# Sliding-window attention and soft mixture of experts on one core: a rewrite with grouped q/k rows, subtracted row maxima, a fixed pipeline of head pairs and column-tiled experts

## The chip, the core and the metric

The kernel runs on one core of a Trainium2 chip (trn2). The core has a matrix engine (TensorE, PE in the profile; its weight loads stand under PEld), a vector engine (DVE), a scalar engine (ACT), GpSimd (POOL) and a queue for transfers (SP). Transfers between the chip's memory (HBM) and the core's SBUF run on 16 DMA engines. Matmul results land in PSUM, which has 8 banks of 2 KB for each of 128 partitions. The metric is the device time of one execution in microseconds (us); the number that counts is the median of several runs.

## The reference

Two stages in a row. Eight batches of eight heads, 576 positions, 64 channels:

```python
scores = scale * np.matmul(q, k.transpose(0, 1, 3, 2))
rel = pos[:, None] - pos[None, :]
mask = (rel >= 0) & (rel < 64)
scores = np.where(mask, scores, -1000000000.0)
scores = scores - np.max(scores, axis=-1, keepdims=True)
attn = np.exp(scores)
attn = attn / (np.sum(attn, axis=-1, keepdims=True) + 1e-09)
out = np.matmul(attn, v)                      # becomes x: 4608 rows of 512
```

Each position sees itself and the 63 positions before it. Then a soft mixture with 32 slots, four for each of 8 experts (512 -> 1024 -> 512):

```python
logits = x @ phi                              # 4608 x 32
d = np.exp(logits - logits.max(0)); d /= d.sum(0) + 1e-09
slot_input = d.T @ x                          # 32 x 512, sums over all 4608 rows
h = np.maximum(slot_input[e] @ w1[e], 0.0)    # 4 rows of each expert
slot_out[e] = h @ w2[e]
c = np.exp(logits - logits.max(1, keepdims=True)); c /= c.sum(1, keepdims=True) + 1e-09
return c @ slot_out                           # 4608 x 512, float32
```

No expert can start before every batch's attention is done, since `slot_input` sums over all rows.

## The kernel before

The work is done in fp16 with fp32 sums. It goes through one loop over the batches `b` and, inside, over four pairs of heads `hp`; a scheduler of the framework orders the instructions of each engine by their dependencies.

Loading: q, k and v of a batch come by GpSimd's queue, each as five transfers (one for each 128 positions, lines 212 and 219), a row of 64 channels being a run of its own: 256 bytes of fp32 in HBM, 128 bytes of fp16 in SBUF. The buffers `q_bf`, `k_bf`, `v_aug`, `v_shf` exist twice. `v_shf` is a copy of `v_aug` moved by 64 positions, made by two transfers within SBUF from SP's queue (lines 223 and 226); the blocks of 64 queries with even index need it, because their 128 keys straddle two of `v_aug`'s groups.

A head pair: `stage_tr` turns q and k so that channels lie on partitions, with plain matmuls against an identity (lines 97 to 109), and ACT and DVE move the results to `qT` and `kT` (lines 105, 106, 111, 112). `stage_qk` multiplies 9 blocks of 128 keys with 64 queries for each head (line 122); ACT takes the exponential with the scale (lines 126 to 129), with no maximum subtracted, and DVE multiplies with a 0/1 mask (lines 127, 130). `stage_av` multiplies with v and a column of ones (lines 146, 148), whose result is the sum of the row; DVE divides (lines 151, 152) into `x_b`. It runs one pair late, from the list `pending`.

Mixture, front: `moe_front_a` and `moe_front_b` for the batch before run at the second and third pair: x is transposed (line 164), multiplied with phi (173, 175), put through the exponential without a maximum (177, 178), transposed back (185) and multiplied with x (198); DVE adds the result to `slotnum`. The exponentials themselves stay in `dnumT`; one over each row's sum stays in `crcp`.

Experts: weights of five experts fit at a time; loads of experts 0 to 4 are issued after batches 3 to 7, and experts 5 to 7 are loaded inside the expert loop, as buffers come free. Each expert has eight 512-column matmuls with four rows of slots (line 276), a rectifier, eight small transposes (285) and eight 512-column matmuls into `sop` (291). Every expert writes to the same low partitions of PSUM.

Output: for each group of 128 rows one matmul (line 301), ACT or DVE with the scale `crcp` (303, 306) into one of two buffers `ob`, and one large and one small transfer a batch (309, 311).

Of the kernel before, what the change touches and what calls it, by code (L numbers as in the profile page):

```python
# [13 lines left out]
AXX = mybir.AxisListType.X  # L14


@with_exitstack
def kernel(
# [15 lines left out]
    SPE = NSLOT // E  # L34
    NB = S // 64
    NC = (S + 127) // 128
    NHD = D // 128
    NFC = F // 128
    scale = 1.0 / float(Dh) ** 0.5

    const = ctx.enter_context(tc.tile_pool(name="const", bufs=1))
    psum = ctx.enter_context(tc.tile_pool(name="psum", bufs=8, space=bass.MemoryType.PSUM))
    pin = ctx.enter_context(tc.tile_pool(name="pin", bufs=2))
    pw = ctx.enter_context(tc.tile_pool(name="pw", bufs=4))
    pxb = ctx.enter_context(tc.tile_pool(name="pxb", bufs=2))
    pxt = ctx.enter_context(tc.tile_pool(name="pxt", bufs=4))
    pmo = ctx.enter_context(tc.tile_pool(name="pmo", bufs=1))
    pex = ctx.enter_context(tc.tile_pool(name="pex", bufs=5))
    pet = ctx.enter_context(tc.tile_pool(name="pet", bufs=2))
    pou = ctx.enter_context(tc.tile_pool(name="pou", bufs=2))  # L50

    ident_f = const.tile([128, 128], FP32, name="ident_f")
    make_identity(nc, ident_f)
    ident_h = const.tile([128, 128], FP16, name="ident_h")
    make_identity(nc, ident_h)

    mask0 = const.tile([128, 64], FP16, name="mask0")
    nc.gpsimd.memset(mask0, 1.0)
    nc.gpsimd.affine_select(
        out=mask0, in_=mask0, compare_op=ALU.is_ge, fill=0.0,  # L60
        base=-1, pattern=[[-1, 64]], channel_multiplier=1,
    )
    nc.gpsimd.affine_select(
        out=mask0, in_=mask0, compare_op=ALU.is_ge, fill=0.0,
        base=64, pattern=[[1, 64]], channel_multiplier=-1,
    )
    mask_bA = mask0[:, :].unsqueeze(1).broadcast_to([128, 4, 64])
    mask_bB = mask0[:, :].unsqueeze(1).broadcast_to([128, 5, 64])

    phi_sb = const.tile([128, NHD, NSLOT], FP16, name="phi_sb")  # L70
    nc.gpsimd.dma_start(out=phi_sb, in_=moe_phi.rearrange("(c p) s -> p c s", p=128))

    dnumT = pmo.tile([32, B, S], FP16, name="dnumT")
    dsums = pmo.tile([32, B + 1], FP32, name="dsums")
    slotnum = pmo.tile([32, D], FP32, name="slotnum")
    slot_inT = pmo.tile([128, NHD, NSLOT], FP16, name="slot_inT")
    slot_oa = pmo.tile([32, D], FP16, name="slot_oa")
    crcp = pmo.tile([128, B, NC], FP32, name="crcp")
    dinv = pmo.tile([32, 1], FP32, name="dinv")

    w1_t = {}
    w2_t = {}

    def load_expert(e):
        w1s = pex.tile([128, NHD, F], FP16, name="w1s", tag="w1s")
        w2s = pex.tile([128, NFC, D], FP16, name="w2s", tag="w2s")
        nc.gpsimd.dma_start(out=w1s, in_=moe_w1[e].rearrange("(c p) f -> p c f", p=128))  # L87
        nc.gpsimd.dma_start(out=w2s, in_=moe_w2[e].rearrange("(c p) d -> p c d", p=128))
        w1_t[e] = w1s
        w2_t[e] = w2s  # L90

    def stage_tr(b, hp, q_bf, k_bf, small):
        h0 = 2 * hp
        qT = pw.tile([128, S], FP16, name="qT", tag="qT")
        kT = pw.tile([128, 64 + S], FP16, name="kT", tag="kT")
        nc.vector.memset(kT[:, 0:64], 0.0)
        nc.tensor.matmul(small[:, 0, :], q_bf[0:64, 4, h0:h0 + 2, :], ident_h[0:64, 0:64],
                         start=True, stop=True)
        nc.tensor.matmul(small[:, 1, :], k_bf[0:64, 4, h0:h0 + 2, :], ident_h[0:64, 0:64],
                         start=True, stop=True)  # L100
        tq = psum.tile([128, 512], FP32, name="tq", tag="ps")
        for c in range(4):
            nc.tensor.matmul(tq[:, 128 * c:128 * c + 128], q_bf[:, c, h0:h0 + 2, :],  # L103
                             ident_h[:, :], start=True, stop=True)
        nc.scalar.copy(out=qT[:, 512:576], in_=small[:, 0, :])  # L105
        nc.scalar.copy(out=qT[:, 0:512], in_=tq[:, :])  # L106
        tk = psum.tile([128, 512], FP32, name="tk", tag="ps")
        for c in range(4):
            nc.tensor.matmul(tk[:, 128 * c:128 * c + 128], k_bf[:, c, h0:h0 + 2, :],  # L109
                             ident_h[:, :], start=True, stop=True)  # L110
        nc.vector.tensor_copy(out=kT[:, 576:640], in_=small[:, 1, :])
        nc.vector.tensor_copy(out=kT[:, 64:576], in_=tk[:, :])  # L112
        return qT, kT

    def stage_qk(qT, kT, small):
        pms = []
        for hl in range(2):
            r0 = 64 * hl
            sA = psum.tile([128, 8, 64], FP32, name="sA", tag="ps")
            for i in range(NB):  # L120
                dst = sA[:, i, :] if i < 8 else small[:, 2 + hl, :]
                nc.tensor.matmul(dst, kT[r0:r0 + 64, 64 * i: 64 * i + 128],  # L122
                                 qT[r0:r0 + 64, 64 * i: 64 * i + 64],
                                 start=True, stop=True)
            pmt = pw.tile([128, NB, 64], FP16, name="pmt", tag="pmt")
            nc.scalar.activation(pmt[:, 0:4, :], sA[:, 0:4, :], AF.Exp, scale=scale)  # L126
            nc.vector.tensor_tensor(out=pmt[:, 0:4, :], in0=pmt[:, 0:4, :], in1=mask_bA, op=ALU.mult)  # L127
            nc.scalar.activation(pmt[:, 4:8, :], sA[:, 4:8, :], AF.Exp, scale=scale)  # L128
            nc.scalar.activation(pmt[:, 8, :], small[:, 2 + hl, :], AF.Exp, scale=scale)
            nc.vector.tensor_tensor(out=pmt[:, 4:9, :], in0=pmt[:, 4:9, :], in1=mask_bB, op=ALU.mult)  # L130
            pms.append(pmt)
        return pms

    def stage_av(b, hp, pms, v_aug, v_shf, x_b):
        for hl in range(2):
            h = 2 * hp + hl
            pmt = pms[hl]
            av = psum.tile([128, 512], FP32, name="av", tag="ps")
            avv = av[:, 0:NC * 65].rearrange("p (c x) -> p c x", x=65)
            for i in range(NB):  # L140
                if i % 2 == 1:
                    rhs = v_aug[:, h, (i - 1) // 2, 0:65]
                else:
                    rhs = v_shf[:, h, i // 2, 0:65]
                r0b = 64 * (i % 2)
                nc.tensor.matmul(av[r0b: r0b + 64, 65 * (i // 2): 65 * (i // 2) + 65],  # L146
                                 pmt[:, i, :], rhs, start=True, stop=True)
            nc.tensor.matmul(av[64:128, 65 * 4: 65 * 4 + 65], pmt[:, 8, :],  # L148
                             v_aug[:, h, 0, 0:65], start=True, stop=True)
            rc = pw.tile([128, NC], FP32, name="rc", tag="rc")  # L150
            nc.vector.reciprocal(rc[:, 0:NC], avv[:, 0:NC, 0])  # L151
            nc.vector.tensor_tensor(  # L152
                out=x_b[:, 0:NC, 64 * h: 64 * h + 64], in0=avv[:, 0:NC, 1:65],
                in1=rc[:, 0:NC].unsqueeze(2).broadcast_to([128, NC, 64]), op=ALU.mult)

    def moe_front_a(b, x_b):
        smx = psum.tile([128, NHD, 64], FP32, name="smx", tag="ps")
        xTs = []
        for kk in range(NHD):
            tx = psum.tile([128, 512], FP32, name="tx", tag="ps")  # L160
            for c in range(NC):
                pn = 128 if c < 4 else 64
                dst = tx[:, 128 * c:128 * c + 128] if c < 4 else smx[:, kk, :]
                nc.tensor.matmul(dst, x_b[0:pn, c, 128 * kk: 128 * kk + 128],  # L164
                                 ident_h[0:pn, 0:pn], start=True, stop=True)
            xT = pxt.tile([128, S], FP16, name="xT", tag="xT")
            nc.scalar.copy(out=xT[:, 0:512], in_=tx[:, :])  # L167
            nc.scalar.copy(out=xT[:, 512:576], in_=smx[:, kk, :])
            xTs.append(xT)
        ltA = psum.tile([128, 512], FP32, name="ltA", tag="ps")  # L170
        ltB = psum.tile([128, 64], FP32, name="ltB", tag="ps")
        for kk in range(NHD):
            nc.tensor.matmul(ltA[0:32, :], phi_sb[:, kk, :], xTs[kk][:, 0:512],  # L173
                             start=(kk == 0), stop=(kk == NHD - 1))
            nc.tensor.matmul(ltB[0:32, :], phi_sb[:, kk, :], xTs[kk][:, 512:576],
                             start=(kk == 0), stop=(kk == NHD - 1))
# [4 lines left out]
    def moe_front_b(b, x_b):  # L181
# [18 lines left out]
        if b == 0:  # L200
            nc.vector.tensor_copy(slotnum[0:32, :], dps[0:32, :])
        else:
            nc.vector.tensor_add(slotnum[0:32, :], dps[0:32, :], slotnum[0:32, :])
# [138 lines left out]
```

## Time and profile before

| | |
|---|---|
| median of 3 runs | 296.59 us (295.79 to 297.07) |
| span of the profiled execution | 291.3 us |
| median less the span | 5.3 us |
| up to the end of the last batch's front | 0 to 212.0 us |
| experts | 212.0 to 259.7 us |
| output | 259.7 to 291.3 us |
| busy | PE 200.2, DVE 126.2, ACT 123.7, POOL 116.1 us |
| instructions | 5506, of them 2080 matmuls |
| HBM | 61.93 MB read, 9.44 MB written |

The span runs from the first to the last instruction of one profiled execution; launching and ending are outside it. Only medians of whole runs are compared. "Busy" adds up the durations of instructions, which overlap on PE. An engine can be idle for two thirds of the time and still set the end in a stage where others wait for it. The profile also shows the share of its full clock that TensorE was granted: it moves between 0.5 and 1.0 in this kernel, and before 49 us there is no record of it (the column then reads 1.00).

### The profile page before, as it was taken

How to read it: one execution, taken by the hardware profiler on the slowest of the kernel's cores; microseconds unless marked ns; L12 is line 12 of the kernel's file. 1: busy time of each engine (PE TensorE's matmuls, PEld its weight loads, DVE VectorE, ACT ScalarE, POOL GpSimd, SP SyncE). 2: the span in 40 equal slices, each digit the busy share in tenths (PEclk: the TensorE clock that was granted, in tenths of full speed). 3: DMA queues.
4: the chain of work that ended last, by engine and by line, in shares of the span. 5: the costliest groups of instructions: out<-in, count | busy, mean ns of one | idle time of the engine just before them, and what ended most of it. 6: DMA issues, size and time to landing. Idle time of an engine off the chain costs nothing.

```text
span 291.3 us, 5506 instructions
## 1 busy us (share of the span) xinstructions
PE 200.2 (69%) x2080; PEld 114.1 (39%) x2080; DVE 126.2 (43%) x459; ACT 123.7 (42%) x403; POOL 116.1 (40%) x148
## 2 busy tenths in 40 slices
PE   0231858757983974996786598598878996685850
PEld 0120745544562552654454456354433432221100
DVE  1030871971682594378189068357320000023331
ACT  1030555553463653635465345464502332144552
POOL 9999396255486471838636380000003300000000
PEclk9999999955555885555596555575669999596555
DMA  7999999999999999999999999900006999909997
GB/s 42 138 114 184 106 165 142 161 216 162 114 182 188 116 208 205 143 143 188 146 140 208 176 128 170 207 6 2 0 0 102 186 210 211 160 0 318 348 362 268
DMA packets 135338, 45.62 MB, mean 157 GB/s; under 512 B 113808, under 2 KB 126096, under 8 KB 135312
## 3 DMA queue, kind: packets, MB, share of 16 engines
q0 software_dynamic: 125584, 30.97, 145.4%
q1 hardware_dynamic: 9728, 14.31, 16.5%
q8 instruction: 16, 0.26, 0.4%
q14 instruction: 10, 0.08, 0.1%
HBM read 61.93 MB, written 9.44 MB: 245 GB/s over the span
## 4 chain that ended last, share of the span: by engine, by line
DMA 29%; PE 22%; issue 20%; POOL 12%; DVE 7%; ACT 7%; ACTq 0%; DVEq 0%; SPq 0%; POOLq 0%
DMA v_shf<-v_aug 14%; DMA w1s<-in_moe_w_dram 7%; DMA out_dram<-ob 5%; POOL v_aug L219 4%; PE tx L164 4%; DMA v_aug<-in_v_dram 3%; PE av L146 3%; PE ltA L173 3%; POOL k_bf L212 3%; POOL q_bf L212 3%; ACT ob L303 3%; PE sA L122 2%; PE dps L198 2%; DVE kT L112 2%; ACT pmt L128 1%
## 5 line engine op out<-in xcount | busy, mean ns | idle before, releaser
L146 PE MATMUL av<-v_shf,pmt 128*64 128x65 f16 x320 | 30.9, 239 | 41.1 <-DMA v_shf<-v_aug 37.8
L212 POOL DMA_DIRECT2D q_bf<-in_q_dram x40 | 33.7, 873 | 32.1 <-PE tq L103 15.2
L126 ACT ACTIVATE pmt<-sA 128x256 f16<-128x256 f32 x64 | 24.8, 388 | 48.9 <-PE small L122 37.9
L212 POOL DMA_DIRECT2D k_bf<-in_k_dram x40 | 34.0, 874 | 21.2 <-DMA w2s<-in_moe_w_dram 12.4
L146 PEld LDWEIGHTS <-pmt 128*64 128x64 f16 x576 | 22.3, 140 | 50.3 <-issue 30.4
L219 POOL DMA_DIRECT2D v_aug<-in_v_dram x40 | 33.7, 871 | 8.0 <-DMA k_bf<-in_k_dram 2.6
L122 PEld LDWEIGHTS <-kT 64*128 64x128 f16 x576 | 23.6, 113 | 22.6 <-issue 10.8
L167 ACT CAST xT<-tx 128x512 f16<-128x512 f32 x32 | 18.1, 591 | 31.6 <-PE tx L164 31.6
L122 PE MATMUL sA<-qT,kT 64*128 64x64 f16 x512 | 25.9, 223 | 6.5 <-DVE kT L112 6.5
L146 PE MATMUL av<-v_aug,pmt 128*64 128x65 f16 x256 | 29.2, 241 | 0.0
L151 DVE RECIPROCAL rc<-av 128x5 f32<-128x5 f32 x64 | 9.6, 176 | 44.5 <-PE av L148 44.1
L152 DVE TENSOR_TENSOR x_b<-av,rc 128x320 f16<-128x320 f32 x64 | 28.2, 479 | 0.1
L112 DVE CAST kT<-tk 128x512 f16<-128x512 f32 x32 | 21.7, 679 | 13.2 <-PE tk L109 12.7
L128 ACT ACTIVATE pmt<-sA 128x256 f16<-128x256 f32 x64 | 25.0, 390 | 0.0
L87 POOL DMA_DIRECT2D w1s<-in_moe_w_dram x8 | 6.1, 768 | 47.1 <-PE hj L276 46.8
L306 DVE TENSOR_SCALAR ob<-cps,crcp 128x512 f32<-128x512 f32 x16 | 11.2, 745 | 29.9 <-PE cps L301 17.9
L127 DVE TENSOR_TENSOR pmt<-pmt,mask_95 128x256 f16<-128x256 f16 x64 | 18.5, 289 | 13.0 <-ACT pmt L126 12.2
L109 PE MATMUL tk<-ident_h,k_bf 128*128 128x128 f16 x128 | 22.5, 281 | 2.1 <-DMA k_bf<-in_k_dram 2.1
L276 PE MATMUL hj<-w1s,slot_inT 128*4 128x512 f16 x64 | 19.8, 428 | 5.9 <-DMA w1s<-in_moe_w_dram 5.5
L106 ACT CAST qT<-tq 128x512 f16<-128x512 f32 x32 | 19.5, 610 | 9.3 <-PE tq L103 9.3
L130 DVE TENSOR_TENSOR pmt<-pmt,mask_95 128x320 f16<-128x320 f16 x64 | 20.7, 323 | 3.6 <-ACT qT L105 0.3
L301 PE MATMUL cps<-slot_oa,dnumT 32*128 32x512 f16 (+1 forms) x40 | 15.9, 508 | 7.4 <-ACT ob L303 6.7
(72 smaller groups left out, 345.9 us busy)
## 6 DMA issues: line engine op xcount, KB each, us to landing
w1s<-in_moe_w_dram POOLq DMA_DIRECT2D x8, 1024.0 KB, 12.6
w2s<-in_moe_w_dram POOLq DMA_DIRECT2D x8, 1024.0 KB, 17.0
out_dram<-ob SPq DMA_DIRECT2D x8, 1024.0 KB, 4.5
q_bf<-in_q_dram POOLq DMA_DIRECT2D x32, 128.0 KB, 6.8
k_bf<-in_k_dram POOLq DMA_DIRECT2D x32, 128.0 KB, 8.0
v_aug<-in_v_dram POOLq DMA_DIRECT2D x32, 128.0 KB, 8.3
v_shf<-v_aug SPq DMA_DIRECT2D x8, 330.0 KB, 6.7
v_shf<-v_aug SPq DMA_DIRECT2D x8, 264.0 KB, 8.2
```

Source lines behind the costliest of these rows:

```text
L106: nc.scalar.copy(out=qT[:, 0:512], in_=tq[:, :])
L109: nc.tensor.matmul(tk[:, 128 * c:128 * c + 128], k_bf[:, c, h0:h0 + 2, :], ident_h[:, :], start=True, stop=True)
L112: nc.vector.tensor_copy(out=kT[:, 64:576], in_=tk[:, :])
L122: nc.tensor.matmul(dst, kT[r0:r0 + 64, 64 * i: 64 * i + 128], qT[r0:r0 + 64, 64 * i: 64 * i + 64], start=True, stop=True)
L126: nc.scalar.activation(pmt[:, 0:4, :], sA[:, 0:4, :], AF.Exp, scale=scale)
L128: nc.scalar.activation(pmt[:, 4:8, :], sA[:, 4:8, :], AF.Exp, scale=scale)
L130: nc.vector.tensor_tensor(out=pmt[:, 4:9, :], in0=pmt[:, 4:9, :], in1=mask_bB, op=ALU.mult)
L146: nc.tensor.matmul(av[r0b: r0b + 64, 65 * (i // 2): 65 * (i // 2) + 65], pmt[:, i, :], rhs, start=True, stop=True)
L152: nc.vector.tensor_tensor(out=x_b[:, 0:NC, 64 * h: 64 * h + 64], in0=avv[:, 0:NC, 1:65], in1=rc[:, 0:NC].unsqueeze(2).broadcast_to([128, N ...
L212: nc.gpsimd.dma_start(out=t_bf[0:pn, c], in_=t_dram[b, :, 128 * c: 128 * c + pn, :].rearrange("h p d -> p h d"))
L219: nc.gpsimd.dma_start(out=v_aug[0:pn, :, c, 1:65], in_=v[b, :, 128 * c: 128 * c + pn, :].rearrange("h p d -> p h d"))
L276: nc.tensor.matmul(hj[0:SPE, :], slot_inT[:, dc, SPE * e: SPE * e + SPE], w1s[:, dc, 512 * j: 512 * j + 512], start=(dc == 0), stop=(dc == ...
```

## The change

The whole body is rewritten, with the order of the instructions written out by hand (`manual_schedule`): each engine runs them in the order of the program.

- q and k of a batch are loaded by one transfer each. A partition holds six consecutive positions, so that a run is 6 x 64 channels. They are turned by 24 transposes in transpose mode a pair, alternating between the two heads' halves of PSUM, and ACT puts the columns back into order while it copies (to `qT` with the scale, and to `kT`).
- v is loaded as before; the shifted copy is made by two GpSimd copies a batch (`shift_v`) in place of the two transfers.
- A row maximum is subtracted. `st_max` computes the scores a first time, queries on partitions: a mask table `wm` is put into PSUM by a 480-column matmul with the identity, 18 small matmuls a head add the scores (32 queries with 96 keys each, on tiles of 64 rows and 32 columns), and DVE takes the maxima. `st_shift` transposes the 10 columns of maxima to rows. `st_score` computes the scores a second time, keys on partitions; five matmuls a head with the table `lh` and the operand `rt` first put mask and negative maximum into the same PSUM bank. ACT then takes the exponential straight into fp16, and no mask multiplication follows.
- The pipeline works on pair `n`: transposes of pair n, maxima of n-1, their turning of n-2, scores of n-3, product with v of n-4. The mixture's front is cut into four parts, one in each step, eight pairs behind.
- Both softmaxes of the mixture subtract maxima: the one over rows by a running maximum with a rescaled sum (`fr_logits`, `fr_slots`), the one over slots after a DVE transpose of the logits (`fr_combine`). A chain of small operations combines four partial statistics at the end.
- Weights of seven experts stay resident and are loaded one a batch from batch 0; the eighth is loaded when the attention's buffers are free.
- Experts: four experts at a time run on the four 32-column tiles of the array, all 32 slots through each expert, and a mask `emask` keeps the four that belong to it.
- The combination weights are normalised beforehand, so the output's copies have no scale; there are four buffers `ob`.
- PSUM: six banks rotate for all of this, two belong to the product with v.

```diff
+    def load_qk(b):
+        qs = pin.tile([G6, H, R6 * Dh], FP16, name="qs", tag="qs")
...
+        nc.gpsimd.dma_start(out=qs, in_=q[b].rearrange("h (g j) d -> g h (j d)", j=R6))
+        nc.gpsimd.dma_start(out=ks, in_=k[b].rearrange("h (g j) d -> g h (j d)", j=R6))
...
+    def shift_v(b):
+        v1, v2 = v1s[b % 2], v2s[b % 2]
+        nc.gpsimd.tensor_copy(out=v2[0:64, :, 1:5, 1:65], in_=v1[64:128, :, 0:4, 1:65])
+        nc.gpsimd.tensor_copy(out=v2[64:128, :, 0:4, 1:65], in_=v1[0:64, :, 0:4, 1:65])
...
+    def st_transpose(p):
+        b, hp = divmod(p, HP)
+        qs, ks = staged[b]
+        for src, dst, sc in ((qs, qTs[p % NQ][:, :], scale), (ks, kTs[p % NQ][:, 64:64 + S], 1.0)):
+            tp = bank([128, R6, G6], FP16, "tp")
+            for j in range(R6):
+                for hl in range(2):
+                    nc.tensor.transpose(tp[64 * hl:64 * hl + 64, j, :],
+                                        src[:, 2 * hp + hl, Dh * j:Dh * j + Dh], ident_h[0:G6, 0:G6])
+            nc.scalar.activation(dst.rearrange("p (g j) -> p j g", j=R6), tp[:, :, :], AF.Copy, scale=sc)
...
+    def st_max(p):
+        qT, kT = qTs[p % NQ], kTs[p % NQ]
+        m = pw.tile([128, 10], FP16, name="m", tag="m")
+        mx = [bank([128, 5, 96], FP32, "mx") for _ in range(2)]
+        for hl in range(2):
+            nc.tensor.matmul(mx[hl][:, :, :], ident_h[:, :], wm[:, :, :], start=True, stop=False,
+                             skip_group_check=True)
+        for c in range(5):
+            for t in range(4 if c < 4 else 2):
+                o = 32 * (4 * c + t)
+                for hl in range(2):
+                    r = slice(64 * hl, 64 * hl + 64)
+                    nc.tensor.matmul(mx[hl][32 * t:32 * t + 32, c, :], qT[r, o:o + 32], kT[r, o:o + 96],
+                                     start=False, stop=True, skip_group_check=True)
+        for hl in range(2):
+            nc.vector.reduce_max(m[:, 5 * hl:5 * hl + 5], mx[hl][:, :, :], axis=AXX)
...
+    def st_shift(p):
+        ps = bank([128, 128], FP32, "mt")
+        nc.tensor.matmul(ps[64:74, :], mts.pop(p)[:, :], ident_h[:, :], start=True, stop=True)
+        nc.vector.tensor_copy(out=rts[p % NR][64:74, :], in_=ps[64:74, :])
...
+    def st_score(p):
...
+        for hl in range(2):
+            for c in range(4):
+                nc.tensor.matmul(sc[hl][:, 2 * c:2 * c + 2, :], lh[:, 5 * hl + c, :], rt[:, :],
+                                 start=(c == 0), stop=False, skip_group_check=True)
...
+        for hl in range(2):
+            nc.scalar.activation(pt[:, 9 * hl:9 * hl + 8, :], sc[hl][:, :, :], AF.Exp)
...
+    def st_av(p):
...
+        nc.vector.reciprocal(rc[:, :, :], avv[:, :, :, 0])
...
+    def fr_logits(b):
...
+        for kk in range(NKK):
+            for t in range(4):
+                nc.tensor.matmul(lg[32 * t:32 * t + 32, :], phi_sb[:, kk, :], xt[:, kk, 128 * t:128 * t + 192],
+                                 start=(kk == 0), stop=(kk == NKK - 1), skip_group_check=True)
...
+    LAG = 4
+    for n in range(NP + LAG):
+        b, hp = divmod(n, HP)
+        if hp == 0:
+            if 0 < b < B:
+                load_v(b)
+            if b + 1 < B:
+                load_qk(b + 1)
+            if b < NRES:
+                load_expert(b, pwt)
+        if hp == 2 and b < B:
+            shift_v(b)
+        if 0 <= n - 2 < NP:
+            st_shift(n - 2)
+        if n < NP:
+            st_transpose(n)
+        if 0 <= n - 3 < NP:
+            st_score(n - 3)
+        if 0 <= n - 1 < NP:
+            st_max(n - 1)
+        if 0 <= n - 4 < NP:
+            st_av(n - 4)
+        if n >= 8 and n < NP + LAG:
+            fb, fi = divmod(n - 8, HP)
+            if fi == 3:
+                front[3](fb)
+                front[4](fb)
+            else:
+                front[fi](fb)
+    for f in front:
+        f(B - 1)
...
+            for kk in range(NKK):
+                for j in range(4):
+                    nc.tensor.matmul(hh[32 * j:32 * j + 32, :], sit[:, kk, :],
+                                     w1_t[4 * g + j][:, kk, 512 * f2:512 * f2 + 512],
+                                     start=(kk == 0), stop=(kk == NKK - 1), skip_group_check=True)
...
+        for fc in range(NFC):
+            for j in range(4):
+                nc.tensor.matmul(ops[32 * j:32 * j + 32, :], hT[:, fc, 32 * j:32 * j + 32],
+                                 w2_t[4 * g + j][:, fc, :],
+                                 start=(g == 0 and fc == 0), stop=(g == 1 and fc == NFC - 1),
+                                 skip_group_check=True)
```

The counts that follow from it: 4088 matmuls in place of 2080 (1152 of them are the small ones of the maxima, 768 the transposes of q and k), and no transfers within SBUF.

## The prediction

> **What bounds the kernel now.** I first cut the span by stages with the view of busy time by stretches, whose columns are: stretch, its length, PE, PEld, DVE, ACT and POOL busy, granted clock, DMA share, GB/s landed.
>
> ```profile
> 38.60:60.40 21.80, 16.11 (x236) 10.76 (x234) 14.24 (x56) 11.83 (x44) 13.74 (x17) 0.98 2.21 165
> 60.40:85.50 25.10, 19.93 (x236) 12.79 (x232) 14.14 (x56) 12.06 (x44) 13.60 (x18) 0.50 2.07 166
> 212.00:259.70 47.70, 38.23 (x204) 15.46 (x203) 2.20 (x9) 11.72 (x26) 4.91 (x6) 0.86 0.77 133
> 259.70:291.30 31.60, 15.89 (x40) 3.70 (x39) 11.18 (x16) 14.53 (x24) 0.00 (x0) 0.57 0.86 299
> 230.00:240.00 10.00, 10.00 (x59) 4.14 (x58) 0.33 (x2) 3.31 (x7) 0.88 (x1) 1.00 1.17 201
> 10.00:20.00 10.00, 4.74 (x40) 2.62 (x40) 2.77 (x9) 3.17 (x11) 10.00 (x13) 1.00 3.13 123
> ```
>
> The first two rows are two batches: no engine fills them, and the clock differs by two between them. Weights land at 201 GB/s (fifth row), 128-byte runs of q, k, v at 123 (sixth). Then the chain of waits (start, us, what) tells what a batch waits for:
>
> ```profile
> 27.84 10.00 DMA v_aug<-in_v_dram
> ...
> 38.60 5.93 DMA v_shf<-v_aug
> ...
> 60.41 6.89 DMA v_shf<-v_aug
> ```
>
> Every batch passes through v landing and the copy within SBUF; the copies start 23.5 us apart on average (38.60 to 155.92, five batches). So attention is paced by transfers, with PE idle several us a batch. The experts (47.7 us) are 128 512-column matmuls one after another plus late loads; the output moves 9.4 MB at 299 GB/s.
>
> **Prices.** The timeline of PE (start, us from first start to last end) gives rates at both clocks: 83.5 and 84 lie at clock 0.5, 99 and 230 at 1.0.
>
> ```profile
> 83.53 0.61 PE L103 MATMUL tq<-ident_h,q_bf 128*128 128x128 f16 x4
> ...
> 84.56 0.29 PE L109 MATMUL tk<-ident_h,k_bf 128*128 128x128 f16 x1
> 84.78 0.26 PE L146 MATMUL av<-v_shf,pmt 128*64 128x65 f16 x1
> 84.78 0.26 PE L146 MATMUL av<-v_aug,pmt 128*64 128x65 f16 x1
> 84.86 0.24 PE L146 MATMUL av<-v_shf,pmt 128*64 128x65 f16 x1
> ...
> 84.91 0.24 PE L146 MATMUL av<-v_shf,pmt 128*64 128x65 f16 x1
> ...
> 99.05 0.39 PE L109 MATMUL tk<-ident_h,k_bf 128*128 128x128 f16 x4
> ...
> 230.10 1.89 PE L291 MATMUL sop<-w2s,hTr 128*32 128x512 f16 x8
> ```
>
> 128 columns: (0.61 - 0.29)/3 = 0.107 us at half clock, (0.39 - 0.22)/3 = 0.057 at full. 512 columns: (1.89 - 0.38)/7 = 0.216 full, so 0.43 half. Two matmuls on different column halves start together, a pair each 0.055 (half); at 99.37 to 99.68 about 0.045 (full). The 64-row scores of line 122 (13 in 0.66 at 73.50, 13 in 0.45 at 98.11, others between) come to 0.03 and 0.025 each. A change of tile shape costs 0.11: 84.56 to 84.78 is 0.22, less 0.107. For the other engines, the groups (busy, mean ns):
>
> ```profile
> L112 DVE CAST kT<-tk 128x512 f16<-128x512 f32 x32 | 21.7, 679 | 13.2 <-PE tk L109 12.7
> ...
> L106 ACT CAST qT<-tq 128x512 f16<-128x512 f32 x32 | 19.5, 610 | 9.3 <-PE tq L103 9.3
> ...
> L191 DVE TENSOR_REDUCE rsum<-td 128x4 f32<-128x128 f32 x8 | 2.2, 281 | 0.0
> ```
>
> DVE from PSUM: (679 - 281)/384 = 1.04 ns an element, so the 480-element maximum takes 0.65 us. ACT: with line 105 (64 elements, 218 ns) 0.875 ns an element, so 0.67 for 576, 0.60 for 512, 1.06 for 1024.
>
> **A step of the new pipeline (one pair), half / full clock, us.** PE: 24 transposes of 96 columns as 12 column pairs, 0.96 / 0.54; eight table matmuls of 128 columns and two of 64, 0.96 / 0.51; 18 scores 0.54 / 0.45; two mask matmuls of 480, 0.80 / 0.40; 36 small maxima at the 0.027 / 0.025 spacing of the scores, 0.97 / 0.90; 20 of v as 10 pairs, 0.55 / 0.45; the maxima's turning 0.11 / 0.06; seven changes of shape 0.77 / 0.70. Sum 5.66 / 4.01.
>
> The change adds a wait: the turning of pair n-1's maxima opens the next step on PE, so all its transposes and scores stand behind it, and it needs both DVE maxima: 0.24 (end of the last matmul) + 2 x 0.65 + 0.1 = 1.64, of which the product with v and its change of shape (0.66 / 0.55) cover part. Left: 1.0 in a step without front work. Step: 6.65 / 5.05. ACT needs 2 x 0.67 + 2 x 0.60 + 2 x 0.23 = 3.0, DVE 2.5: both fit beneath.
>
> The front per batch on PE: transposes of x 1.93 / 1.03; 16 logit matmuls on four column tiles 0.64 / 0.40, hidden in the 1.0; the last quarter 0.25 + two rounds of 512 columns + ACT's two copies with handoffs, 2.1 / 1.8. Less the 1.0 that each replaces: +2.2 / +1.0. ACT is in order, so front work sits in front of the next pair's qT and kT copies, whose two banks the mask matmuls need: x's copies (2.6 us more in one step), the exponentials that wait for DVE's maximum, and those of the combination. At half clock PE comes late enough; at full clock I put 1.2 + 0.8 + 1.2. Batch: 4 x 6.65 + 2.2 = 28.8 at half, 4 x 5.05 + 1.0 + 3.2 = 24.4 at full.
>
> **The clock** is the largest unknown. The clock was 1.0 right after the densest stretches (the x transposes before 49 and 97, line 291 from 220 on) and 0.5 otherwise, so a PE that works 80% of the time should hold it more often than now. I take full two thirds of the time: 26 us a batch.
>
> [...]
>
> **Transfers per batch.** Weights 2.1 MB at 201 GB/s, 10.4 us; v 0.59 MB at 123, 4.8; q and k 1.18 MB in six times longer runs, between 123 and 201 GB/s, 5.9 to 9.6. Sum 21 to 25 us, beneath 26, and a batch ahead. v_shf's wait goes; GpSimd's copies of 2048 elements (by its selects of 64 and 128 elements, 0.254 us at line 59 and 0.287 for the identity, 0.5 ns an element: 1.3 us each) have two steps, some 12 us, before the product with v asks; beyond 6 us each they would show. What is late next is PE.
>
> **Sum.** Start: GpSimd issues q, k (two at 0.87, row of line 212), identity 0.5, five of v 4.4, eight selects of 480 elements 3.8, the tables 3.3, phi 0.9, so tables at 15; steps 0 to 2 run meanwhile, step 3's scores follow: step 4 starts at 24 (22 to 26). Steps 4 to 31, seven batches: 182. Four emptying steps without transposes: 13. The last front, now alone (12 handoffs; before it took 7 from 204.7): 10. Statistics chain, 14 small operations of 0.15 to 0.4 with handoffs: 5. Experts: 128 matmuls in fours, 32 x 0.216 = 6.9 at full clock, 16 transposes 0.9, rectifiers, copies and handoffs 4: 12 (17 at half clock). Expert 7 (12 us to load) comes during the emptying. Slots combined: 2. Output: 31, since it is the rate of 9.4 MB, 299 GB/s over the stage; four buffers save at most the 2 us before the first transfer. 24 + 182 + 13 + 10 + 5 + 12 + 2 + 31 = 279, against 291.3: attention +17, experts -29. With the 5.3 us between span and median: **284 us**.
>
> Four column tiles at once are not in the trace, only two. Ends: full overlap as taken, or none beyond the pairs. In pairs the experts take 7 more.
>
> [...]
>
> **Rivals.**
> - *PE stays at half clock* (slower). Place: the attention loop, where the wait for the maximum in every step keeps PE from being dense enough. 7 x 28.8 = 202, the other parts 25, 15, 10, 6, 17, 3, 31: 309 + 5 = 314. It decides from 27.8 us a batch on. For it: clock 0.50 through 25 us with PE busy 19.9 (second row). Against: PE's idle gaps there are 4 us and more, here 1.
> - *PE runs at full clock* and transfers pace the loop at 23 to 24.4: 7 x 24 + 22 + 12 + 9 + 5 + 11 + 2 + 30 = 259 + 5 = 264. For it: the clock at 1.0 from 220 to 247.
> - *Small column tiles don't overlap*: 36 maxima at 0.08 / 0.04 add 1.9 / 0.5 a step, about 1 at the mix, 4 x 7 = 28, and the experts 7 to 20: near 325. Against: the paired starts at 84.78.
> - *The rewrite keeps the old pace* (v's landing still last, 23.5 a batch): 262 + 5 = 267, near the second rival and counted with it.
>
> **Chances.** Forecast (272 to 296) 0.43, half clock 0.25, full clock or transfer pace 0.22, no overlap 0.10. A measurement of this kernel tells 0.5% (1.5 us) from no change. Faster: 0.22 and most of the forecast's, 0.60; within: 0.05; slower 0.35. The range leaves out a tenth on each side: 256 to 320; the forecast's own is 272 to 296.
>
> **What would show it** (lines of the new kernel). Starts of L212 (the turning) 24 to 29 us apart by four, idle 0.5 to 1 before it released by DVE's line 207; granted clock 0.7 to 0.9 in the loop; L204 25 to 27 ns apart; experts under 15 us. Wrong if L94's copies or q's landing release PE, if ACT's strided copies (line 190) exceed 1 us, since ACT then becomes the bound, or if PE's issue is slower than the 25 ns spacing.

## The result and the profile after

The changed kernel is slower: 376.41 us median (375.44 to 377.36) beside 296.31 (295.79 to 297.07) for the kernel before in the same runs, a ratio of 1.270 [1.263, 1.278]. Medians are of all runs, and ratios, here and below, leave out runs more than 1.5% above the fastest of their kernel. The forecast was 284, and the range ended at 320. The profiled execution spans 374.8 us.

From the page of the changed kernel: busy time of the engines, then the shares of the chain that ended last by engine and by line, then two groups of instructions (busy us, mean ns of one, idle us before them and what ended it).

```profile
PE 224.8 (60%) x4091; PEld 142.8 (38%) x4091; DVE 137.3 (37%) x335; ACT 213.7 (57%) x311; POOL 99.8 (27%) x111
...
ACT 37%; PE 27%; DVE 18%; issue 8%; DMA 4%; POOL 2%; DVEq 0%; ACTq 0%; POOLq 0%
...
L190 ACT ACTIVATE qT<-tp 128x576 f16<-128x576 f16 x32 | 67.0, 2093 | 41.5 <-PE tp L188 41.3
L190 ACT ACTIVATE kT<-tp 128x576 f16<-128x576 f16 x32 | 73.3, 2290 | 1.5 <-PE tp L188 1.5
```

The mean duration in the last two rows (2093 and 2290 ns) decides: a copy of q or k takes 2.09 or 2.29 us. The prediction had 0.67. The largest share of the chain is ACT's, at 57% busy time; PE is busier and holds less of it.

The view of busy time by stretches (columns as in the prediction) of the changed kernel, for steps 4 to 31, emptying with the last front and the statistics, experts, and output:

```profile
42.00:293.50 251.50, 169.99 (x3366) 115.30 (x3366) 92.89 (x217) 167.68 (x234) 70.19 (x67) 0.65 0.95 102
293.50:326.40 32.90, 18.95 (x301) 12.52 (x300) 18.00 (x50) 12.68 (x36) 1.66 (x2) 0.60 0.39 65
326.40:341.40 15.00, 11.40 (x145) 4.79 (x146) 1.50 (x2) 4.70 (x9) 0.00 (x0) 0.83 0.01 1
341.40:374.80 33.40, 13.14 (x40) 2.79 (x39) 12.40 (x20) 10.27 (x20) 0.00 (x0) 0.56 0.84 283
```

The loop takes 251.5 us, 35.9 a batch; the transfers move only 102 GB/s in it, so they wait for it and not it for them. Experts and output are near what was forecast.

One step of that loop, from the timeline of the changed kernel (start, duration, engine, line, what; in brackets the idle time before it and what ended that):

```profile
154.38 0.22 PE L212 MATMUL mt<-ident_h,m 128*10 128x128 f16 x1
...
155.62 2.12 ACT L190 ACTIVATE qT<-tp 128x576 f16<-128x576 f16 x1
...
157.33 2.32 ACT L190 ACTIVATE kT<-tp 128x576 f16<-128x576 f16 x1
157.79 0.56 PE L197 MATMUL mx<-wm,ident_h 128*128 128x480 f16 x1 [1.43 <-ACT qT L190]
...
159.70 0.56 PE L197 MATMUL mx<-wm,ident_h 128*128 128x480 f16 x1 [1.35 <-ACT kT L190]
...
160.19 0.59 PE L204 MATMUL mx<-kT,qT 64*32 64x96 f16 x36
...
162.10 0.27 PE L212 MATMUL mt<-ident_h,m 128*10 128x128 f16 x1
```

The two mask matmuls need the PSUM banks that the copies read. PE has been ready since 156.36, and stands 1.43 us for qT's copy and 1.35 for kT's. In other places of the loop the table matmul of the last block of keys (line 225) waits for these copies too. From the view of line 190 in the changed kernel, who waited for them over the whole execution (us in total, times):

```profile
  PE s L225: 37.9, 26
  PE mx L197: 30.9, 29
```

Together PE stands 68.8 us for the copies. This was the prediction's own condition ("Wrong if … ACT's strided copies (line 190) exceed 1 us, since ACT then becomes the bound").

The start is late too. From the timeline of the changed kernel:

```profile
17.31 0.09 DVE L104 MEMSET v<- 128x32 f16 x1 [17.31 <-DMA v<-in_v_dram]
...
19.41 0.60 POOL L119 TENSOR_SCALAR_AFFINE_SELECT wm<-wm 32x480 f16<-32x480 f16 x1 [11.67 <-DVE wm L116]
...
24.79 0.96 PE L197 MATMUL mx<-wm,ident_h 128*128 128x480 f16 x2 [12.10 <-POOL wm L121]
```

v's ones are written behind the issue of v's first loads, into the same buffers; DVE waits 17.31 us for the landing, GpSimd's mask selects stand 11.67 us behind DVE, and PE's first mask matmul 12.10 behind those. Step 4 (the turning of pair 2) starts at 42.0, not 24.

Against the forecast of 279 for the span: start +18, seven batches of 35.93 in place of 26 +69.5, emptying, front and statistics 32.9 in place of 28, experts and slots 15.0 in place of 14, output 33.4 in place of 31. That is 279 + 18 + 69.5 + 8.3 = 374.8, the whole span.

### The profile page after: what moved, and what is told of

Its sections match the earlier page's. It is cut to its first block, busy times and chain, and to the rows that moved or that the text cites. A ratio compares the mean times of both kernels' runs of the same rounds, so it can differ in the third digit from the quotient of the medians.

```text
span 374.8 us, 9146 instructions
## 1 busy us (share of the span) xinstructions
PE 224.8 (60%) x4091; PEld 142.8 (38%) x4091; DVE 137.3 (37%) x335; ACT 213.7 (57%) x311; POOL 99.8 (27%) x111
## 4 chain that ended last, share of the span: by engine, by line
ACT 37%; PE 27%; DVE 18%; issue 8%; DMA 4%; POOL 2%; DVEq 0%; ACTq 0%; POOLq 0%
ACT kT L190 16%; ACT qT L190 13%; DVE m L207 6%; PE mx L197 6%; PE mx L204 5%; DMA out_dram<-ob 4%; ACT xt L277 4%; DVE x_b L259 3%; PE av L252 3%; PE tx L275 2%; PE tp L188 2%; PE hh L432 1%; DVE ob L471 1%; PE si L342 1%; PE si L344 1%
## 5 line engine op out<-in xcount | busy, mean ns | idle before, releaser
L207 DVE TENSOR_REDUCE m<-mx 128x5 f16<-128x480 f32 x64 | 39.1, 654 | 149.0 <-PE mx L204 149.0
L190 ACT ACTIVATE qT<-tp 128x576 f16<-128x576 f16 x32 | 67.0, 2093 | 41.5 <-PE tp L188 41.3
L190 ACT ACTIVATE kT<-tp 128x576 f16<-128x576 f16 x32 | 73.3, 2290 | 1.5 <-PE tp L188 1.5
L87 POOL DMA_DIRECT2D v<-in_v_dram x32 | 28.1, 894 | 123.9 <-PE td L332 113.2
L197 PE MATMUL mx<-wm,ident_h 128*128 128x480 f16 x64 | 33.3, 562 | 43.5 <-ACT kT L190 24.0
L234 ACT ACTIVATE pt<-sc 128x512 f16<-128x512 f32 x64 | 39.7, 676 | 8.0 <-PE s L231 7.9
L225 PE MATMUL s<-rt,lh 75*128 75x64 f16 x64 | 12.5, 219 | 43.3 <-ACT qT L190 29.4
L222 PE MATMUL sc<-rt,lh 75*128 75x128 f16 x256 | 29.8, 289 | 0.0
L259 DVE TENSOR_TENSOR x_b<-av,rc 128x640 f16<-128x640 f32 x32 | 26.4, 825 | 1.1
L252 PE MATMUL av<-v,pt 128*64 128x65 f16 x576 | 23.5, 242 | 3.4 <-DVE x_b L259 3.4
L222 PEld LDWEIGHTS <-lh 75*128 75x128 f16 x256 | 22.2, 130 | 3.5 <-issue 0.2
```

The source lines that it names most:

```text
L87: nc.gpsimd.dma_start(out=v1[:, :, c, 1:65], in_=v[b, :, 128 * c:128 * c + 128, :].rearrange("h p d -> p h d"))
L190: nc.scalar.activation(dst.rearrange("p (g j) -> p j g", j=R6), tp[:, :, :], AF.Copy, scale=sc)
L197: nc.tensor.matmul(mx[hl][:, :, :], ident_h[:, :], wm[:, :, :], start=True, stop=False, skip_group_check=True)
L207: nc.vector.reduce_max(m[:, 5 * hl:5 * hl + 5], mx[hl][:, :, :], axis=AXX)
L222: nc.tensor.matmul(sc[hl][:, 2 * c:2 * c + 2, :], lh[:, 5 * hl + c, :], rt[:, :], start=(c == 0), stop=False, skip_group_check=True)
L234: nc.scalar.activation(pt[:, 9 * hl:9 * hl + 8, :], sc[hl][:, :, :], AF.Exp)
```

## The experiments

Ratios are against the kernel before, run beside each version. A letter in an expectation stands for a theory; A is that ACT's stepped copies set the pace of the loop. "A batch" below is a seventh of the time from step 4 to step 32.

### What in the copy is slow

The copy reads 96 neighbouring columns of PSUM for each of six j and writes them 6 elements (12 bytes) apart. First the reordering alone was left out: q and k stay in the order of the transposes, so masks and products meet the wrong positions, with as much work.

```diff
-            nc.scalar.activation(dst.rearrange("p (g j) -> p j g", j=R6), tp[:, :, :], AF.Copy, scale=sc)
+            nc.scalar.activation(dst.rearrange("p (j g) -> p j g", j=R6), tp[:, :, :], AF.Copy, scale=sc)
```

> The copies to qT and kT write their 576 columns in the order in which they read them, one after the other, instead of 6 columns (12 bytes) apart; the reordering of the positions is left out, everything else stays. Theory A (the 12-byte step of the write makes ACT's copy 2.1 to 2.3 us in place of the 0.67 forecast, and the loop waits for these copies): L190 takes 0.65 to 0.75 us, a step falls from 9.0 to about 6, and 28 steps times 3 take 70 to 90 us off: 285 to 305 us. Theory B (the copy is slow for what it reads, fp16 in PSUM next to a writing PE): L190 stays above 1.5 us and the time above 350. Theory C (the loop is bound by the round trip of the maximum, PE to DVE to PE, and the copies only fill its wait): L190 falls, but the steps stay above 8 us and the time above 350.

Measured 310.82 us, 1.049 [1.029, 1.069]; 27.1 us a batch; the copy 0.65 us. A stands; B (the copy is slow for what it reads) and C (the maximum's round trip holds the steps above 8 us) fall, since a step is now 6.8 us on average.

Then the step was moved to the read of PSUM: the write is contiguous, the read takes one element of each j in turn, 192 bytes apart. This computes what the changed kernel computes.

```diff
+            nc.scalar.activation(dst.rearrange("p (g j) -> p g j", j=R6), tp[:, :, :].rearrange("p j g -> p g j"), AF.Copy, scale=sc)
```

> The same columns, but ACT's copy now writes contiguously and takes the step on its read from PSUM (192 bytes apart). Theory A, with the cost on the writing side alone: L190 near 0.7 us and the time near that of the run without reordering, 285 to 305 us. If a step costs as much on either side: L190 at 2 us or more and the time near 376. Theory B: above 1.5 us and above 350.

312.18 us, 1.054 [1.037, 1.070]; 26.9 a batch. From the group view of this kernel for line 190 (shortest, median and longest in ns):

```profile
L190 ACT ACTIVATE qT<-tp x32: 632/650/684, 8.1 to 223.1; 128x576 f16<-128x576 f16 x32
L190 ACT ACTIVATE kT<-tp x32: 642/645/685, 11.1 to 223.6; 128x576 f16<-128x576 f16 x32
```

Same 576 elements, same order in the result, 0.65 us: the read's step costs nothing, the write's step 1.4 to 1.6 us. One line gives back 64 us of the 80.

Third, kT's copy on DVE with the write's step kept:

```diff
+            if sc == 1.0:
+                nc.vector.tensor_copy(out=dst.rearrange("p (g j) -> p j g", j=R6), in_=tp[:, :, :])
+            else:
+                nc.scalar.activation(dst.rearrange("p (g j) -> p j g", j=R6), tp[:, :, :], AF.Copy, scale=sc)
```

> The copy to kT moves from ACT to DVE, with its 12-byte step; ACT keeps qT's. Theory A (ACT's time in the loop is the bound: 2 x 2.2 + 2 x 0.68 + 2 x 0.24 = 6.2 us a pair and the front's 1.2): ACT loses 2.3 us a step, DVE gains 0.7 (if DVE writes with a step at its usual 1.04 ns an element) to 2.3, a step falls to 6.7 to 7.5, time 310 to 335 us. Theory C (round trip of the maximum): DVE sits in that trip, so the time stays at 376 or rises.

343.72 us, 1.160 [1.147, 1.173]; 30.9 a batch: the right direction, above the range. The same view of line 191 (the DVE copy):

```profile
L191 DVE COPY kT<-tp x32: 2060/2074/2198, 28.9 to 255.0; 128x576 f16<-128x576 f16 x32
```

DVE takes 2.07 us for it, where line 112 of the kernel before took 0.68 for 512 elements written contiguously. So DVE pays the step as ACT does, and the load was shared and not removed. The expectation had allowed for that price; what put the time above its range was not taken apart.

### The late start

```diff
-    load_v(0)
     for i in range(2):
         nc.vector.memset(v1s[i][:, :, :, 0], 1.0)
...
+    load_v(0)
```

> The memsets of the ones and zeros beside v are written ahead of the first load of v, so that they don't wait for it; the loop is as in the changed kernel. Theory: the start lost 17 us because DVE's first memset waited until 17.3 us for v to land and the mask table's selects on GpSimd waited for DVE's memset behind it: step 4 starts near 28 in place of 42 us, time 376 less 11 to 16: 360 to 365 us. Rival (the start is bound by GpSimd's own selects and issues, and by ACT's slow first copies): time falls by less than 6 us, over 370.

364.54 us, 1.230 [1.219, 1.242]; step 4 at 30.3 in place of 42.0, batches unchanged at 36.0. The whole gain at the start reaches the end (11.9 us).

### Both repairs

> The changed kernel with both repairs at once: the copies write contiguously and step on the PSUM read instead, and v's ones are written ahead of v's first transfers. If the two losses are separate terms (loop 64 us, start 12 us), the time is 312 - 12 = 300 us: 296 to 304, with batches of 27 us still and step 4 at 30 us. If the late start was partly hidden by the slow loop or the other way about, it stays above 305.

301.39 us (299.22 to 301.81), 1.019 [1.011, 1.026], step 4 at 28.7, 27.1 a batch. The two losses are separate terms and add up. What is left of the late start shows in this kernel's timeline:

```profile
13.12 2.97 DVE L157 COPY ss<-ident_h 32x128 f16<-32x128 f16 x4
...
16.23 1.28 DVE L167 TENSOR_REDUCE emask<-ident_h 32x1 f32<-32x4 f16 x8
...
18.81 0.27 PE L212 MATMUL mt<-ident_h,m 128*10 128x128 f16 x1 [4.20 <-DVE m L207]
```

DVE fills two tables that only the tail needs (`ss`, `emask`) before it takes the first maxima, and PE stands 4.20 us for the maxima.

The rest of this section starts from this kernel. One steady step without front work, from its timeline:

```profile
40.31 0.27 PE L212 MATMUL mt<-ident_h,m 128*10 128x128 f16 x1 [0.63 <-DVE m L207]
...
40.52 0.69 PE L188 MATMUL tp<-ident_h,qs 96*64 96x96 f16 x12
...
41.62 1.03 PE L222 MATMUL sc<-rt,lh 75*128 75x128 f16 x8
...
46.10 0.27 PE L212 MATMUL mt<-ident_h,m 128*10 128x128 f16 x1 [0.63 <-DVE m L207]
```

A step is 46.10 - 40.31 = 5.79 us, 0.63 of it the wait for the maximum. The eight table matmuls take 1.03: (1.03 - 0.27)/7 = 0.109 each, the price of half clock, while the profile's column of the granted clock reads 1.00 here. It reads 1.00 from the start until it falls at 69 us, although matmuls of the same size show half clock until about 53 us (the eight tables take 1.03 again at 47.40). The duration of a matmul of known size is the safer clock.

### What the second score pass costs

The max pass and its turning are left out, so no maximum is subtracted, as in the kernel before.

```diff
-        if 0 <= n - 2 < NP:
-            st_shift(n - 2)
...
-        if 0 <= n - 1 < NP:
-            st_max(n - 1)
```

> As the kernel with both repairs, but the row-maximum pass and its turning are left out (the mask table's row of maxima stays zero, so the softmax is computed without subtracting a maximum, as in the kernel before). This measures what the second score pass costs. Theory PE: per step the pass is 0.8 + 0.6 + 0.1 us of PE work, two changes of shape and the wait for the maximum of 0.5 to 1, 2.2 to 2.9 us, so a batch falls from 27 to 15.5 to 18 us and the time from 300 to 220 to 240. Rival: the transfers of 21 to 25 us a batch, until now beneath, become the pace: 255 to 285, with PE's or GpSimd's waits ended by v, q and k landing. Rival: ACT is the bound already, with 2 x 0.65 + 2 x 0.6 + 2 x 0.23 = 3.0 us a step and 5 of front a batch: hardly a change, above 285.

273.33 us (271.02 to 275.64), 0.922 [0.914, 0.931]: the fastest version of all, ahead of both kernels (it leaves out what the changed kernel adds for the maximum). From its waits (engine, what waited, what for: us in total, times, longest):

```profile
PE tp L188 <- DMA qs<-in_q_dram: 34.0, 7, 8.1
PE tp L188 <- DMA ks<-in_k_dram: 16.7, 8, 2.9
```

The rival came true: with the pass gone, PE waits 51 us for q and k. From the first table matmul to the last (16.8 to 202.7 us, 31 pairs apart) a batch is 24.0 us, within the 21 to 25 of the prediction's transfers. So the pass costs about 28 us of time (301.4 - 273.3); its own 2.2 to 2.9 us a step would be 62 to 81 over 28 steps, but the transfers stop the gain.

### The wait for the maximum

The turning comes one step later, and scores, product with v and front behind it.

```diff
-        if 0 <= n - 2 < NP:
-            st_shift(n - 2)
+        if 0 <= n - 3 < NP:
+            st_shift(n - 3)
...
-    LAG = 4
+    LAG = 5
```

> As the kernel with both repairs, but the maxima's turning comes one step later (and with it the scores and the product with v), so that a whole step lies between the maximum on DVE and the matmul that asks for it. If the wait for the maximum costs its 0.5 to 1.0 us a step on the path, 28 steps give back 14 to 28 us less the one step of emptying added (3 us): 275 to 290. Rival: the time passes to the next wait (scores for the copies of ACT, exponentials for the scores): within 5 us of the kernel with both repairs.

334.45 us, 1.133 [1.126, 1.141]: a miss with a cause of its own. The load of v for batch b was still issued at the batch's first step, ahead of the last product that reads that buffer for batch b-2; that product got the new v and waited for it, so this version does not compute the reference. The waits of this kernel show it:

```profile
PE av L252 <- DMA v<-in_v_dram: 37.1, 24, 7.6
```

The second try issues the loads at the end of that step:

> The later turning once more, with the loads of v, q, k and weights issued at the end of the batch's first step instead of at its beginning, so that v's buffer is no longer overwritten before the last product that reads it and that product waits for no landing. In the kernel with both repairs a step without front work takes 5.79 us with matmuls at half clock, 0.63 of it PE idle for the maximum, and the batch 26.7. If the wait for the maximum is a cost on the path, the batch falls by 4 x 0.63 = 2.5 us and a little more where PE gets dense enough for the full clock: 7 x 2.5 to 4 less 3 for the longer emptying: 274 to 288. Rival: transfers and the hold of ACT by the front take its place: 295 to 303.

298.09 us (294.62 to 299.55), 1.000 [0.995, 1.004], 26.5 a batch: about 2% better than 1.019, less than expected and inside the rival's 295 to 303. The wait for the maximum is gone from PE's list, and others stand there. From the waits of PE in this kernel:

```profile
PE s L225 <- ACT d L303: 12.6, 6, 3.5
PE s L225 <- ACT qT L190: 10.4, 11, 1.6
PE tp L188 <- DMA qs<-in_q_dram: 10.2, 2, 7.3
PE tp L188 <- DMA ks<-in_k_dram: 6.7, 3, 2.7
```

With both repairs alone the first two were 6.7 and 5.8, and the maximum's 14.5. So part of what the maximum gave back went to waits for ACT: for the front's exponentials (L303) and for q's copies. The two waits are 23.0 us now, 12.5 before.

### The front's place

```diff
             st_transpose(n)
+        if n >= 8 and n < NP + LAG:
+            fb, fi = divmod(n - 8, HP)
...
         if 0 <= n - 3 < NP:
             st_score(n - 3)
```

> As the kernel with both repairs, but a step's front work stands right behind the transposes of the step and not at its end, so on ACT it comes behind the copies of q and k and not in front of the next ones. If the front's hold on those copies costs its 1.2 + 0.8 + 1.2 us a batch, the time falls by 7 x 1 to 3 us: 280 to 294. Rival: the front's exponentials that wait for DVE then hold up the exponentials of the scores, which the product with v asks for: no change or some us more, 298 to 306.

306.30 us, 1.034 [1.026, 1.043], 27.8 a batch: no gain, as the rival said, at the upper end of its range. PE's wait for the maximum grew from 14.5 to 29.3 us, since no front work stands ahead of the turning any more. Whether the front's exponentials also hold up those of the scores, as the expectation put it, no row separates.

### The clock

Two useless matmuls of 480 columns in each step, just ahead of the turning:

```diff
-        ps = bank([128, 128], FP32, "mt")
+        ps = bank([128, 480], FP32, "mt")
+        for _ in range(2):
+            nc.tensor.matmul(ps[:, :], ident_h[:, :], wm[:, :, :].rearrange("p c x -> p (c x)"), start=True, stop=True)
```

> As the kernel with both repairs, with two useless matmuls of 128x128 weights and 480 columns in each step, in the place where PE waits for the maximum; they take 0.8 us at half clock, 0.4 at full. Theory that the clock is low because of the idle gap of 0.6 us in each step: the clock rises to 1.0 for most of the loop, the step falls below 5.3 and the time to 275 to 295 in spite of more work. Rival that such gaps are not what decides: the clock stays and the work adds 0.2 us in steps with a gap and 0.8 in those without: 310 to 325.

and the same with 32x32 weights (`ident_h[0:32, 0:32]`, `wm[0:32]`):

> The same two useless matmuls, but with 32x32 weights: as many columns and as long on PE, on a sixteenth of the array. If the clock follows PE's idle time alone, the time is that of the version with 128x128 weights within 5 us. If it follows how much of the array works, this one stays at half clock and is slower than that one by 10 us or more.

In time they are unclear: 301.19 us (292.79 to 303.73) and 305.58 (301.68 to 308.42), beside 301.39 for both repairs at another time, and the first one's median lies between its two forecasts, its fastest run in the lower one. Their early steps are clear. The table matmuls at about 30 us, from the timelines, first with 128x128 weights:

```profile
27.04 0.22 PE L214 MATMUL mt<-ident_h,m 128*10 128x128 f16 x1 [0.82 <-DVE m L207]
...
31.34 0.22 PE L214 MATMUL mt<-ident_h,m 128*10 128x128 f16 x1
32.12 0.62 PE L224 MATMUL sc<-rt,lh 75*128 75x128 f16 x8
```

then with 32x32 weights:

```profile
28.73 0.27 PE L214 MATMUL mt<-ident_h,m 128*10 128x128 f16 x1 [0.42 <-DVE m L207]
30.03 1.03 PE L224 MATMUL sc<-rt,lh 75*128 75x128 f16 x8
```

0.62 is full clock ((0.62 - 0.22)/7 = 0.057 each), 1.03 half. These steps last 4.1 us with the large weights, 5.8 to 6.0 with the small, 5.79 with none, although both fill the same place. Nor are the gaps smaller where the clock is full: with the large weights PE stands 0.82 us for the maximum at 27.04, with the small ones 0.42 at 28.73. In all, the eight tables run at full clock in 7 of 32 steps of the changed kernel and 11 of 32 with both repairs; of the steps where the view shows them as one block, in 20 of 30 with the large weights and 11 of 31 with the small. Over the whole execution the mean granted clock is 0.72 to 0.77 in the four runs with the large weights and 0.68 to 0.72 in the four with the small. So in these traces it isn't the small idle gaps that keep the clock low; the size of the added weights decides, which speaks for how much of the array works. That the time hardly moves fits the extra work of 0.4 to 0.8 us a step and the steps with front work, which still take about 8 us in both.

Last, the later turning and the large matmuls together:

> The later turning together with the two useless 128x128 matmuls in each step. Alone, the later turning left batches of 26 to 28 us with the tables of 18 of 32 steps at full clock; the useless matmuls alone raised that from 11 to 20. If the clock and the wait for the maximum were all that kept the loop above the pace of the transfers, both together give steps of 4.0 us without front work (3.6 + 0.4) and the loop falls to the 22 to 24 us a batch of the transfers: 270 to 285. Rival: the front's hold of ACT (steps of 8.06 us in both) sets the batch, and the time stays at 293 to 303.

0.989 [0.980, 0.998] of the kernel before, 296.71 us median; tables at full clock in 22 of 32 steps. The time is the rival's. One late batch, step by step, from the view of busy time by stretches:

```profile
178.29:186.10 7.81, 5.29 (x114) 3.08 (x113) 4.09 (x13) 3.66 (x11) 0.09 (x1) 0.78 1.16 208
186.10:194.20 8.10, 6.49 (x122) 3.28 (x121) 5.87 (x13) 3.10 (x9) 2.17 (x3) 0.70 0.49 74
194.20:201.17 6.97, 6.97 (x134) 5.05 (x134) 2.46 (x5) 3.58 (x8) 2.02 (x3) 0.61 1.82 81
201.17:205.64 4.47, 4.25 (x130) 2.77 (x129) 1.55 (x4) 3.45 (x8) 3.63 (x2) 1.00 0.01 4
```

The rival's reason is half of it. In the first two steps PE is idle for 2.5 and 1.6 us, and 3.9 us of this batch are waits for ACT (for the front's exponentials, q's copies and the copy of the turned exponentials). The third step has no idle time on PE at all and lasts 6.97 us at a clock of 0.61. So what remains above the transfers is the front's hold of ACT and PE's own work below full clock.

## Why the prediction was wrong

- **The step that failed** is the price of the copies: "ACT needs 2 x 0.67 + 2 x 0.60 + 2 x 0.23 = 3.0, DVE 2.5: both fit beneath". The 0.875 ns an element came from line 106 of before, a copy with a contiguous write, and was put on one whose write steps by 12 bytes. The copies measured 2.09 (qT) and 2.29 us (kT) in place of 0.67. ACT's 3.0 a step became about 6, PE waited for it twice a step, and 7 x 9 = 63 us of the 80 between the kernels follow (312 in place of 376 with this one thing changed). The working named 1 us as the limit and gave no chance to what lies beyond it.
- What the write's step costs is shown for 12 bytes alone, 2.1 to 2.3 us against 0.65. No run here tried another step on the write.
- **Start**, forecast 24: 42.0. The queue was counted by issues alone; v's ones wait for a transfer issued before them, and the masks stand behind them on DVE and then on GpSimd. 11.7 of the 18 us are that wait, and 1.6 the slow copies (28.7 with both mended). Of the 4.7 left, some 3 are DVE's tables, which the working left out: by an estimate, the first maxima's matmuls end at 14.6 and the two maxima take 1.2, so without them the turning could start near 16 and not at 18.81. The rest stays open.
- **Batch**, forecast 26: 26.9 to 27.1 once the copies are mended, but two errors cancel. The clock was taken full two thirds of the time and was full in a third of the steps (11 of 32), so the rival *PE stays at half clock* had the state right. The step was priced at 6.65 at half clock and is 5.79 (the wait 0.63 for 1.0, the small maxima 0.52 for 0.97 up to the next matmul), so the rival's 28.8 a batch was too long. The first row of the prediction (0.98 in the batch from 38.60) was also read as a clock, in part ahead of any record: at 40.22 us line 103 of the kernel before takes 0.61 us for four matmuls, the price of half clock.
- The coupling through ACT (1.2 + 0.8 + 1.2 = 3.2 a batch at full clock) is real and near its size: 3.9 us in the late batch of the last version.
- **Transfers**, 21 to 25 us a batch hidden beneath the step: right, and shown by the version without the max pass, which falls on them at 24.0. GpSimd's copies of v took 1.91 us (forecast 1.3), and in the changed kernel nothing waited for lines 94 and 95.
- **Column tiles**: right. The rival without overlap is refuted by 36 small maxima in 0.59 us (0.009 each from start to start, forecast 0.025 to 0.027) and by the experts below.
- **Experts** 12, with slots 14: 15.0, half clock for the first third. **Output** 31: 33.4. Emptying, front and statistics 28: 32.9.

With both repairs the kernel gives 301.4, 6% from the forecast, and still 1.9% slower than the kernel before: the late start's remainder (5 us), 7 x 1.1 in the loop and 8 in the tail.

## What to carry to other kernels

Price a copy by its element count only where a row of the profile has the same access pattern; where a reorder can stand on the read of PSUM or on the write to SBUF, try it on the read: here that was free (0.65 us a copy, where the step on the write took 2.1 to 2.3). Before buffers are initialised, look at what has been issued into them: an initial write behind a load waits for the landing (here 17.31 us), and so does all that is queued behind it (GpSimd's selects 11.67 us, PE's first mask matmul 12.10). After removing a wait, look which engine's queue the next one sits in: here the later turning gave about 2%, the front's other place cost 5 us and the added matmuls gave nothing clear, until the work itself was left out and the transfers became the pace.

## What the runs showed of the hardware

- A step of 12 bytes on the SBUF write makes a 576-element fp16 copy take 2.06 to 2.34 us on ACT and 2.06 to 2.20 on DVE; 0.65 on ACT without it; a step of 192 bytes on the PSUM read costs nothing (0.65 as well).
- Four column tiles overlap fully here, 32 matmuls of 512 columns in 1.90 us at full clock. From the timeline of the changed kernel, experts at half and at full clock:

```profile
326.46 3.60 PE L432 MATMUL hh<-w,sit 128*32 128x512 f16 x32 [0.35 <-ACT sit L423]
...
333.95 1.90 PE L432 MATMUL hh<-w,sit 128*32 128x512 f16 x32
```

  32 matmuls in fours are eight rounds: (1.90 - 0.38)/7 = 0.217 a round, the 0.216 of a single 512-column matmul at full clock, so a steady run of four tiles gives four times the rate of one.
- With both repairs the clock stayed at half through early steps whose idle gaps on PE are 0.63 us (the eight tables 1.03 us at 41.62). It rose early when two 128x128 matmuls of 480 columns were added to a step, with gaps up to 0.82 us left (the tables 0.62 at 32.12), and not with 32x32 ones (1.03 at 30.03; one trace of each).
